# A fused attention and mixture-of-experts kernel: v in the layout of k and q, a new order of the attention steps, and the routed stage written out as an ordered list

## The chip, the cores and the metric

The kernel runs on one core of a Trainium2 chip. The metric is device time in microseconds (us) of one execution, as the median of three runs. Five engines work beside each other: TensorE (PE; its weight loads are shown apart as PEld), VectorE (DVE), ScalarE (ACT), GpSimd (POOL) and SyncE (SP), which here only issues DMAs.

## The reference

The output of an attention layer goes through two mixture-of-experts layers. Inputs are random, in float32.

```python
# attention: 4 batches, 8 heads, S = 576, head size 64
scores = q @ k.T / 8 + bias          # bias: a small MLP of relative positions, one table per head
attn = exp(scores - max); attn = attn / (sum(attn) + 1e-9)
x = (attn @ v) with heads side by side       # 2304 tokens x 512

# soft MoE: 8 experts with 4 slots each, w1 512x1024, w2 1024x512
logits = x @ phi                     # 2304 x 32
d = softmax of logits over tokens;   slot_in = d.T @ x        # 32 x 512
slot_out[e] = relu(slot_in[e] @ w1[e]) @ w2[e]
x = (softmax of logits over slots) @ slot_out                 # rank 32

# routed MoE: one expert per token, for tokens with x @ w_skip > 0
e = argmax(x @ w_gate); g = its softmax weight
out = x + g * (relu(x @ w1[e]) @ w2[e])
```

After the soft MoE each token is a mixture of 32 slot outputs, x = cT . S4, and the mixing weights cT are kept instead of x. The kernel expects that all routed tokens choose one expert; `code` says whether that holds, and a slower loop stands behind it if it doesn't.

## The kernel before

**Attention** is done in 16 pairs n (two heads, one batch), each in five row tiles t of queries: four of 128 rows, t = 4 being the 64 rows left of both heads. A pair's steps are named in a table. LK, LQ and LV load k, q and v (L333, L338, L346); BA and BM load tiles of the position bias. KHI/KLO and QHI/QLO (GpSimd) split k and q into a high and a low part of reduced precision. KG, QG and LAST transpose them on TensorE (suffix p) and copy them out (suffix e, ScalarE). SW (L423, GpSimd) makes a second copy of k with its halves swapped. QKtj (L451 to L461) makes the scores `sc` of tile t and head j on TensorE, its eviction (L468, VectorE) adds the bias and takes the extreme value `st`, EXtj (L475, ScalarE) the exponential e. For tiles 0 to 2, HI (L486, GpSimd) and LO (L490, VectorE) split e into two float16 halves in a tile `ehl`, and TD (L495) has a DMA issued by SyncE transpose it into eT; AVtj (L576, L580) multiplies eT with v. Tiles 3 and 4 are transposed on TensorE (T3, T4) and multiplied by AVB (L588). For v, LV loads tn with an overlapping access: each partition holds eight rows of 64 numbers of both heads, in two DMAs; VA (L382, L386) copies them, scaled, into tv: one copy of 512 columns over all partitions and two of 64 columns over half of them, for the ninth rows; VH and VLO make its float16 halves v16. N0, N1, NB and N3 divide by the sums and write X, XT and XU transpose it, LG adds to the logits `lgT` (LG, in every second pair, and SA, SB, SC in the last four are the soft MoE's logits and slot sums).

What sets the order: under `manual_schedule` each engine runs its instructions in the order in which the code issues them. The code sorts all steps of all pairs by `n * II + SCHED[step]`, with II = 14100, and by `LAST[step]` in the last four pairs, and issues them in this order, so each engine, and SyncE's queue, has its part of the sorted list. A number of the table reaches the chip only through this order. Sorting starts after the bias tables and a few early steps; the first load in it waits for the last bias load (`lead`).

**The stream.** When the last transpose is issued, SyncE issues the loads of the soft experts' weights (`weight_piece`, L239 and L244, 64 pieces of 512 KB) into a ring of buffers; TensorE multiplies each as it lands. At piece 24 of the second half the kernel guesses the routed expert and loads its weights w1e and w2e, in four quarters each. `w10` holds gate and skip weights; `rk` a table of constants.

**The routed stage** is one straight run of code. It multiplies cT by SW for the gate logits (L1143), and VectorE takes from them the maximum, the mask and the counts of tokens per expert (`cnt`), which TensorE sums (L1153). `slots` (L1070) and `slots_sum` (L1078) multiply the slots' outputs with w1e, `bounds` (L1178) finds for each hidden unit whether it can be positive at all, `x2(t)` (L1092, L1093) writes x of tile t, one product and one copy by ScalarE or VectorE, in nineteen turns. The units that can change sign, at most 128, are gathered: a gather reads their rows of w2 (`W2c`), and `Gc` holds their first layer. The buffers `pg` and `py` hold four PSUM tiles each.

**The last loop** (L1298 to L1308) takes the 18 tiles in groups of four (4, 0, 1, 2, 3): `hid(g)` makes the hidden values of a group, one product (L1275), hhi on ScalarE (L1276) and hlo on VectorE (L1277); it is called one group ahead, before the tiles of the present group. Each tile has four products into y (L1302 to L1305), one addition on VectorE (L1306) and a store in two halves (L1350), one issued by SyncE, one by ScalarE.

Of the kernel before, what the change touches and what calls it, by code (L numbers as in the profile page):

```python
# [20 lines left out]
P = 128  # L21
# [14 lines left out]
SCHED = {"LK": 0, "LQ": 6481, "LV": 18003, "BA": 29213, "BM": 40002, "TD0": 37159, "TD1": 48797, "TD2": 38491,  # L36
         "KHI": 4821, "KLO": 9101, "QHI": 9252, "QLO": 10704, "VA": 21547, "VH": 33628, "VLO": 35392, "KG0p": 14818,
# [11 lines left out]
LAST = {"LK": [1362, -2225, -531, 82], "LQ": [1402, 4025, 6684, 922], "LV": [13529, 24916, 14702, 18622],  # L49
         "BA": [16706, 42343, 32163, 20903], "TD0": [38203, 45142, 33962, 21822], "TD1": [56442, 46262, 35002, 22702],  # L50
         "TD2": [42582, 45222, 33442, 21302], "KHI": [2606, 6011, 10736, 15262], "KLO": [4960, 9316, 11410, 15302],
         "QHI": [7495, 7003, 13862, 15622], "QLO": [11336, 11842, 13902, 15782], "VA": [25094, 28402, 30002, 19382],
# [53 lines left out]
def soft_moe_attention_kernel(ctx, tc, q, k, v, w1, b1, w2, phi, mw1, mw2,  # L106
# [139 lines left out]


    qm_b = [fix.tile([P, 4, 64], F32R, name=f"qm{i}") for i in range(2)]
    tv_b = [fix.tile([P, 5, 2, VD], F32, name=f"tv{i}") for i in range(2)]
    for t in qm_b:  # L250
        pool.memset(t.bitcast(F32), 0.0)
    for t in tv_b:
        pool.memset(t[:, 0:4], VS)
        pool.memset(t[:, 4], 0.0)
        for j in range(2):
            pool.memset(t[j * 64:(j + 1) * 64, 4, j, 64:VD], VS)
# [1148 lines left out]
```

## Time and profile before

| what | value |
| --- | --- |
| three runs: median (lowest to highest) | 488.33 us (487.57 to 489.01) |
| the profiled execution, its own time; its span | 484.54 us; 482.8 us |
| busy, share of the span: PE, DVE, ACT, POOL | 419.8 (87%), 349.5 (72%), 304.9 (63%), 248.0 (51%) us |
| PEld | 309.0 us (64%) |
| DMA | 112.02 MB, 232 GB/s in the mean |
| chain that ended last, by engine | PE 43%, DMA 30%, DVE 7%, ACT 7%, POOL 6% |
| its largest single item | the transposing DMA eT<-ehl, 16% |

The span is the time from the first to the last recorded instruction. Busy times are means over stages with different limits. The chain is followed back from the last instruction, at each step to what released it. A mean granted clock of TensorE of 1.0 is full speed (2.4 GHz), 0.50 is its lower level (1.2 GHz).

### The profile page before, as it was taken

How to read it: one execution, taken by the hardware profiler on the slowest of the kernel's cores; microseconds unless marked ns; L12 is line 12 of the kernel's file. 1: busy time of each engine (PE TensorE's matmuls, PEld its weight loads, DVE VectorE, ACT ScalarE, POOL GpSimd, SP SyncE). 2: the span in 40 equal slices, each digit the busy share in tenths (PEclk: the TensorE clock that was granted, in tenths of full speed). 3: DMA queues.
4: the chain of work that ended last, by engine and by line, in shares of the span. 5: the costliest groups of instructions: out<-in, count | busy, mean ns of one | idle time of the engine just before them, and what ended most of it. 6: DMA issues, size and time to landing. Idle time of an engine off the chain costs nothing.

```text
span 482.8 us, 11572 instructions
## 1 busy us (share of the span) xinstructions
PE 419.8 (87%) x4314; PEld 309.0 (64%) x4314; DVE 349.5 (72%) x825; ACT 304.9 (63%) x635; POOL 248.0 (51%) x243
## 2 busy tenths in 40 slices
PE   4789996999989989979989999987887687989993
PEld 2445666998878978878988878876453211355462
DVE  6999966898896988868979788997564600147564
ACT  3999966988896988868888787874421200037510
POOL 5530018898996997995998799853300000000000
PEclk9989997999998999989999999999999799979998
DMA  6468859999999999999899999689999999890166
GB/s 187 151 217 276 281 189 208 238 209 236 193 224 243 171 216 226 216 197 220 205 210 245 176 194 198 148 152 204 390 392 411 403 394 400 304 330 0 28 202 196
DMA packets 151997, 112.02 MB, mean 232 GB/s; under 512 B 118176, under 2 KB 120736, under 8 KB 151936
## 3 DMA queue, kind: packets, MB, share of 16 engines
q1 hardware_dynamic: 150032, 107.99, 86.5%
q10 hardware_dynamic: 1824, 2.97, 1.8%
q8 instruction: 36, 0.59, 0.5%
q0 software_dynamic: 80, 0.26, 0.2%
q14 instruction: 25, 0.20, 0.1%
HBM read 67.49 MB, written 15.34 MB: 172 GB/s over the span
## 4 chain that ended last, share of the span: by engine, by line
PE 43%; DMA 30%; DVE 7%; ACT 7%; POOL 6%; issue 4%; SPq 1%; ACTq 0%; POOLq 0%; DVEq 0%
DMA eT<-ehl 16%; PE sc L451 8%; PE sc L208 8%; DMA x<-in_moe_w_dram 6%; PE av L580 4%; DMA k<-in_moe_w_dram 2%; DMA bias<-in_moe_w_dram 2%; DVE ehl L490 2%; PE pt L406 2%; DVE xnat L1306 2%; ACT ev L211 2%; POOL k L423 2%; PE av L576 2%; PE pbig L1030 2%; PE pt L686 2%
## 5 line engine op out<-in xcount | busy, mean ns | idle before, releaser
L468 DVE CUSTOM_DVE_ANT_0 e<-sc,bias 128x576 f32<-128x576 f32 x128 | 92.5, 750 | 19.1 <-PE sc L451 18.7
L451 PE MATMUL sc<-k,qT 128*128 128x288 f32 x512 | 97.5, 321 | 7.0 <-DVE st L468 4.8
L475 ACT ACTIVATE e<-e,st 128x576 f32<-128x576 f32 x128 | 96.8, 774 | 6.4 <-DVE st L468 5.8
L486 POOL TENSOR_SCALAR ehl<-e 128x1152 f16<-128x1152 f32 x48 | 63.7, 1331 | 71.1 <-ACT e L475 68.4
L490 DVE SCALAR_TENSOR_TENSOR ehl<-e,ehl 128x1152 f16<-128x1152 f32 x48 | 85.1, 1773 | 5.1 <-POOL ehl L486 5.1
L451 PEld LDWEIGHTS sc<-k,qT 128*128 128x128 f32 x512 | 74.7, 196 | 13.7 <-DVE st L468 7.9
L208 PE MATMUL sc<-hid,w2b 128*32 128x288 f32 x576 | 52.5, 434 | 6.5 <-ACT ev L211 3.7
L204 DVE TENSOR_SCALAR hid<-ll,nib 128x576 f32<-128x576 f32 x117 | 55.6, 557 | 1.4 <-PE sc L208 1.4
L580 PE MATMUL av<-v,eT 128*128 128x65 f16 x1152 | 49.9, 195 | 0.0
L423 POOL TENSOR_SCALAR k<-k 64x1152 fp32r<-64x1152 f32 x30 | 47.2, 1575 | 3.8 <-ACT k L439 1.8
L208 PEld LDWEIGHTS sc<-hid,w2b 128*32 128x32 f32 x576 | 27.5, 114 | 29.4 <-ACT ev L211 12.8
L580 PEld LDWEIGHTS <-eT 128*128 128x128 f16 x1152 | 44.2, 99 | 1.5 <-issue 0.3
L371 POOL TENSOR_SCALAR sk<-tk 128x576 fp32r<-128x576 f32 x16 | 30.4, 1899 | 10.4 <-PE pt L434 4.8
L211 ACT ACTIVATE ev<-sc,offs,ipi 128x576 f32<-128x576 f32 x36 | 29.8, 828 | 6.9 <-PE sc L208 6.6
L588 PE MATMUL av<-eq,tv 128*64 128x192 f32 x320 | 29.5, 331 | 0.0
L1132 POOL TENSOR_SCALAR Lt<-rk 128x128 f16<-128x128 f32 x1 | 0.3, 297 | 56.7 <-DMA sk<-in_moe_w_dram 56.7
L576 PE MATMUL av<-v,eT 128*128 128x130 f16 x144 | 16.5, 224 | 14.3 <-DMA eT<-ehl 14.3
L543 PE MATMUL pt<-ident,e 128*128 128x128 f32 x144 | 24.4, 281 | 2.0 <-ACT e L475 2.0
L997 DVE COPY part<-pbig 128x256 f32<-128x256 f32 x2 | 0.8, 425 | 33.0 <-ACT part L996 33.0
L588 PEld LDWEIGHTS av<-eq,tv 128*64 128x64 f32 x320 | 21.6, 137 | 3.7 <-issue 0.5
L996 ACT COPY part<-pbig 128x256 f32<-128x256 f32 x2 | 0.7, 372 | 36.6 <-PE pbig L1030 36.6
L548 ACT COPY eq<-pt 128x512 f32<-128x512 f32 x32 | 18.7, 586 | 8.0 <-PE pt L543 7.6
(338 smaller groups left out, 883.2 us busy)
## 6 DMA issues: line engine op xcount, KB each, us to landing
scratch<-ev SPq DMA_DIRECT2D x36, 288.0 KB, 3.7
x<-in_moe_w_dram SPq DMA_DIRECT2D x20, 512.0 KB, 10.2
bias<-scratch SPq DMA_DIRECT2D x16, 576.0 KB, 5.2
bias<-in_moe_w_dram SPq DMA_DIRECT2D x17, 512.0 KB, 10.3
tn<-in_v_dram SPq DMA_DIRECT2D x32, 256.0 KB, 5.5
k<-in_moe_w_dram SPq DMA_DIRECT2D x16, 512.0 KB, 10.5
tk<-in_k_dram SPq DMA_DIRECT2D x16, 288.0 KB, 3.1
tq<-in_q_dram SPq DMA_DIRECT2D x16, 288.0 KB, 5.7
```

The lines of the kernel that those rows point to most:

```text
L204: vec.tensor_scalar(out=hid, in0=src, scalar1=nib[:, gi:gi + 1], scalar2=None, op0=ALU.max)
L208: pe.matmul(pb[c * 32:(c + 1) * 32, hh, 0:288], lhsT=w2b, rhs=hid[:, hh * 288:(hh + 1) * 288], start=True, stop=True)
L211: act.activation(ev, pb[:, :, 0:288].rearrange("p a (l u) -> p u a l", u=NU), AF.Identity, bias=offs[not on_act], scale=ipi[:, bt:bt + 1])
L371: pool.tensor_scalar(out=sx[:, :, 0, :], in0=t, scalar1=1.0, scalar2=1.0, op0=ALU.mult, op1=ALU.mult)
L423: pool.tensor_scalar(out=k1[64 * i:64 * i + 64], in0=k0[64 - 64 * i:128 - 64 * i], scalar1=1.0, scalar2=1.0, op0=ALU.mult, op1=ALU.mult)
L451: pe.matmul(sc[:, hh, 0:288], lhsT=l_, rhs=kf[i][:, o:o + 288], start=(i == 0), stop=(i == 1))
L468: vec.tensor_tensor_reduce(out=z["e", t][:, o].rearrange("p (a j) -> p a j", a=2), in0=z.pop(("sc", t, j))[:, :, 0:288], in1=bias_t[hp, t] ...
L475: act.activation(ee, ee, AF.Exp, bias=z["m", t][:, j:j + 1], scale=-1.0, **kw)
L486: pool.tensor_scalar(out=eh[:, 0], in0=z["e", t], scalar1=ES, scalar2=1.0, op0=ALU.mult, op1=ALU.mult)
L490: vec.scalar_tensor_tensor(out=eh[:, 1], in0=z.pop(("e", t)), scalar=ES, in1=eh[:, 0], op0=ALU.mult, op1=ALU.subtract)
L580: pe.matmul(av[:, oj:oj + VD], lhsT=eT[:, ei, 5 * j + c], rhs=v16[:, vi, c, j], start=False, stop=lastt and k_ == 2 and c == 3)
L588: pe.matmul(z["av", 1][j * 64:(j + 1) * 64, o], lhsT=tv[:, c, j, 0:64], rhs=z["eq"][:, 4 * j + c if c < 4 else 8], start=False, stop=last ...
```

## The change

**v.** LV loads v like k and q: one DMA, nine rows of 64 numbers of one head in each partition, 64 partitions for each head. `tv` has ten blocks instead of five times two; VA fills it with four copies over 64 partitions each, two of five rows (320 columns) and two of four (256 columns). VH, VLO and the AV products only index it anew.

```diff
-    tv_b = [fix.tile([P, 5, 2, VD], F32, name=f"tv{i}") for i in range(2)]
+    tv_b = [fix.tile([P, 10, VD], F32, name=f"tv{i}") for i in range(2)]
...
         def LV():
-            tn = new(v_p, [P, 2, 8, 64], F32, "tn", bufs=1)
-            src = v[b, h0, 0, :]
-            for a in range(2):
-                sync.dma_start(out=tn[a * 64:(a + 1) * 64].rearrange("p j u d -> p j (u d)"),
-                               in_=bass.AP(tensor=src.tensor, offset=src.offset + a * 64,
-                                           ap=[[NU * 64, 64], [S * 64, 2], [1, 512]]))
+            sync.dma_start(out=new(v_p, [P, NU, 64], F32, "tn"),
+                           in_=v[b, h0:h0 + 2].rearrange("h (l u) d -> (h l) u d", u=NU))
...
         def VA():
-            tn = z["tn"][:, 0, 0, :]
-            act.activation(tv[:, 0:4, :, 0:64], bass.AP(tensor=tn.tensor, offset=tn.offset,
-                                                        ap=[tn.ap[0], [2 * 64, 4], [9 * 64, 2], [1, 64]]), AF.Copy, scale=VS)
             for j in range(2):
-                i, o = slice(64 - j * 64, 128 - j * 64), slice(j * 64, (j + 1) * 64)
-                act.activation(tv[o, 4, j, 0:64], z["tn"][i, j, 7 - 7 * j], AF.Copy, scale=VS)
+                i, o = slice(j * 64, (j + 1) * 64), slice(64 - j * 64, 128 - j * 64)
+                act.activation(tv[i, 5 * j:5 * j + 5, 0:64], z["tn"][i, 0:NU:2], AF.Copy, scale=VS)
+                act.activation(tv[o, 6 * j:6 * j + 4, 0:64], z["tn"][i, 1:NU:2], AF.Copy, scale=VS)
...
-                    pe.matmul(av[:, oj:oj + VD], lhsT=eT[:, ei, 5 * j + c], rhs=v16[:, vi, c, j],
+                    pe.matmul(av[:, oj:oj + VD], lhsT=eT[:, ei, 5 * j + c], rhs=v16[:, vi, 6 * j + c],
```

**The order of the attention steps.** SCHED and LAST have new numbers throughout; II stays. The entries that are spoken of below:

| step | before | after | | step | before | after |
| --- | --- | --- | --- | --- | --- | --- |
| LQ | 6481 | 0 | | LO0 | 31998 | 29204 |
| LK | 0 | 1320 | | AV00 | 38684 | 41620 |
| LV | 18003 | 1698 | | LO1 | 40817 | 36350 |
| BA | 29213 | 28833 | | AV10 | 49644 | 45586 |
| BM | 40002 | 37041 | | LO2 | 34798 | 28988 |
| TD0 | 37159 | 37204 | | AV20 | 41201 | 38306 |
| TD1 | 48797 | 37353 | | KLO | 9101 | 7086 |
| TD2 | 38491 | 37080 | | KG0p | 14818 | 10835 |

The order on SyncE's queue for one pair of the middle, before (the start of a row is the line, then the operation and its tiles; "bias2" is one of the bias buffers, "ehl" the two halves of a row tile). The three transposes are those of row tiles 1, 0 and 2:

```order
L333 DMA tk_2488<-in_k_dram 128x576
L269 DMA bias2_2503<-scratch_72 128x1152
L346 DMA tn_2549<-in_v_dram 64x2x512 x2
L338 DMA tq_2593<-in_q_dram 128x576
L495 DMA_TRANSPOSE eT_2595<-ehl_2379 128x18x128
L495 DMA_TRANSPOSE eT_2668<-ehl_2505 128x18x128
L495 DMA_TRANSPOSE eT_2690<-ehl_2530 128x18x128
```

and after:

```order
L344 DMA tq_2513<-in_q_dram 128x576
L275 DMA bias2_2518<-scratch_72 128x1152
L339 DMA tk_2534<-in_k_dram 128x576
L349 DMA tn_2547<-in_v_dram 128x576
L495 DMA_TRANSPOSE eT_2690<-ehl_2475 128x18x128
L495 DMA_TRANSPOSE eT_2692<-ehl_2480 128x18x128
L495 DMA_TRANSPOSE eT_2696<-ehl_2561 128x18x128
```

q has gone to the front and v is one load; the transposes still stand in a row behind the loads, now in the order of row tiles 2, 0 and 1.

**The routed stage.** Each piece of code becomes a named step, with the PSUM tile of each kept in a dictionary, and a string `ORDER` says in which order they are issued. w10 moves to another pool, and the product of ST4 with w10 (PW) becomes a step of the stage.

```diff
+ORDER = ("SL0 PW SL1 GP0 SS0 SWt GP1 P4 SW SS1 PL0 GH0 BD0 PL1 S4t SD0 S4 GH1 BD2 SD1 X17 RR2 GB0 PL2 X3 SL2 "
+         "XE17 PL3 GP2 RR0 SL3 SS2 XE3 GP3 MX GB1 BD3 EX GH2 X4 ACTM EA CNT RR3 XE4 LG8 SS3 BD4 SD2 GB2 GH3 X11 "
...
+         "XE9 X5 PN M9 C9 PR EX2 MR2 HOE SLA EXP SLB GE1 YOA PIA FL X10 XE10 PIB POSM GS1 GCE IX EIDX X15 ELIST "
+         "XE5 YOB GS2 GACT GC X13 XE15 X6 GCF MISC PT X0 XE13 YT X7 GATH XE6 BAD XE7 H4 H0 TP H4A H4D W2CH P4B "
+         "X16 W2CL T4T XE16 T4 X18 H0A XE18 PO H0D X12 XE12 XE0 ACCO")
+X2V = (7, 18)
...
-        w10 = sp.tile([P, 4, 10], F32, name="w10")
+        w10 = late.tile([P, 4, 10], F32, name="w10")
...
+    def x2e(t):
+        (vec.tensor_copy if t in X2V else act.copy)(acc[:, t, :] if t < NT else accO, z.pop(("x2", t)))
```

SL, GP, SS, GH, SD and GB are the parts of `slots`, `slots_sum` and `slots_low`; PL the gate products; MX, EX, EA and CNT VectorE's way to the counts, PN their product; BD and RR the bounds and their maxima; X and XE the products and copies of x2, two of the copies on VectorE where there were four. TensorE's order at the start of the stage, before ("pc" and "y" are PSUM tiles, "bias_5706" is ST4):

```order
L1001 MATMUL pc<-sel,part_6329 128x128 x4
L1043 MATMUL pw<-w_6296,bias_5706 128x10 x4
L1140 MATMUL pc<-ident,bias_5706 128x128 x4
L1143 MATMUL y<-SW,bias_6218 128x10 x8
L1143 MATMUL y<-SW,w 128x10 x10
L1143 MATMUL y<-SW,cO 128x10
L1070 MATMUL pc<-w1e,bias_5706 32x256 x4
L1153 MATMUL y<-cnt,ones 128x8
L1070 MATMUL pc<-w1e,bias_5706 32x256 x4
L1078 MATMUL pc<-gp,sel 128x256
L1070 MATMUL pc<-w1e,bias_5706 32x256 x4
```

and after:

```order
L1000 MATMUL pc<-sel,part_6327 128x128 x4
L1070 MATMUL pc<-w1e,bias_5716 32x256 x4
L1157 MATMUL pc<-w_6294,bias_5716 128x10 x4
L1070 MATMUL pc<-w1e,bias_5716 32x256 x4
L1078 MATMUL pc<-gp,sel 128x256
L1167 MATMUL pc<-ident,bias_5716 128x128 x4
L1078 MATMUL pc<-gp,sel 128x256
L1176 MATMUL y<-SW,bias_6216 128x10 x5
L1216 MATMUL pc<-MR,gh 128x512
L1176 MATMUL y<-SW,bias_6216 128x10 x3
L1176 MATMUL y<-SW,w 128x10 x2
L1216 MATMUL pc<-MR,gh 128x512
```

The slots' products with w1e now come first, the gate products follow in four pieces, and the product of cnt (L1153 before) is no longer among them: counted from the last product with `part` it was the 7th row and is the 35th.

**The last loop.** `hid` is cut in three, `hid_p` (the product), `hid_a` (hhi) and `hid_d` (hlo); for groups 4 and 0 all three stand in ORDER (H4, H4A, H4D, H0, H0A, H0D). The products and hhi of a group are called two groups ahead, hlo behind the second tile of a group.

```diff
-            for g in (4, 0, 1, 2, 3):
-                if g != 3:
-                    hid((g + 1) % 5)
+            groups = (4, 0, 1, 2, 3)
+            for i, g in enumerate(groups):
+                ahead = groups[i + 2] if i < 3 else None
+                if i < 3:
+                    hid_p(ahead)
+                    hid_a(ahead)
                 for t in range(4 * g, min(4 * g + 4, NT)):
...
                     store((sync, act), out, acc, t)
+                    if i < 3 and t % 4 == 1:
+                        hid_d(ahead)
```

ScalarE's order as it enters the loop, before:

```order
L1093 COPY xnat<-y 128x512 x6
L1291 TENSOR_LOAD code
L1292 COMPARE_AND_BRANCH
L1276 ACTIVATE hhi<-pc 128x512
L1350 DMA out_dram<-xnat 64x512 x2
L1276 ACTIVATE hhi<-pc 128x512
L1350 DMA out_dram<-xnat 64x512 x4
L1276 ACTIVATE hhi<-pc 128x512
```

and after:

```order
L1327 ACTIVATE hhi<-pc 128x512
L1103 COPY xnat<-y 128x512 x2
L1356 TENSOR_LOAD code
L1357 COMPARE_AND_BRANCH
L1327 ACTIVATE hhi<-pc 128x512
L1419 DMA out_dram<-xnat 64x512 x2
L1327 ACTIVATE hhi<-pc 128x512
L1419 DMA out_dram<-xnat 64x512 x4
```

In the loop before, the rows are hhi of group 0, two stores of group 4, hhi of group 1, four stores of group 0, hhi of group 2. After, hhi of group 0 stands in the routed stage, and hhi of group 1 ahead of the stores of group 4, that of group 2 ahead of those of group 0: each is one group further ahead of its tiles.

## Rows read from the trace of the kernel before

**Rows 1.** Busy time by stretch (us; instructions in brackets), granted clock, DMA share, GB/s.
```profile
core 0: us, PE busy (x) PEld busy (x) DVE busy (x) ACT busy (x) POOL busy (x), PEclk, DMA share, GB/s
104.20:255.70 151.50, 139.94 (x1661) 125.89 (x1660) 127.30 (x306) 124.64 (x275) 131.29 (x109) 0.98 1.06 214
255.70:336.60 80.90, 72.62 (x880) 63.10 (x878) 70.27 (x168) 61.65 (x138) 61.24 (x52) 1.00 0.94 185
336.60:420.20 83.60, 67.78 (x579) 28.02 (x581) 29.11 (x75) 13.72 (x37) 4.96 (x25) 0.96 1.03 390
424.10:455.10 31.00, 28.61 (x165) 15.40 (x164) 19.70 (x58) 17.15 (x39) 3.19 (x9) 0.89 0.33 117
455.10:476.20 21.10, 18.70 (x76) 13.95 (x76) 14.71 (x22) 3.49 (x7) 0.00 (x0) 1.00 0.59 180
```

**Rows 2.** The same view, three single attention pairs.
```profile
154.70:170.50 15.80, 15.77 (x193) 14.49 (x192) 14.39 (x34) 14.33 (x32) 14.01 (x12) 1.00 0.98 183
170.50:187.30 16.80, 14.87 (x183) 13.17 (x183) 13.95 (x36) 13.40 (x31) 15.06 (x13) 1.00 1.12 230
203.10:223.20 20.10, 17.36 (x194) 15.73 (x192) 14.23 (x34) 14.01 (x32) 14.95 (x13) 0.92 1.13 234
```

**Rows 3.** TensorE's waits, 104.2 to 255.7 us: total, times, longest.
```profile
PE av L576 <- DMA eT<-ehl: 9.3, 6, 2.7
PE sc L451 <- POOL k L423: 1.2, 1, 1.2
PE sc L451 <- DVE st L468: 0.7, 1, 0.7
```

**Rows 4.** The tile eT: who waited, and DMA time to landing.
```profile
  PE av L576: 14.3, 12
DMA to landing us min/median/max: 4.5/5.3/9.5
```

**Rows 5.** Timeline of SyncE's queue: start, us, line, tiles, count.
```profile
204.21 12.59 SPq L495 DMA_TRANSPOSE eT<-ehl  x3
216.89 0.54 SPq L333 DMA_DIRECT2D tk<-in_k_dram  x1
217.48 0.41 SPq L269 DMA_DIRECT2D bias<-scratch  x1
218.00 1.29 SPq L346 DMA_DIRECT2D tn<-in_v_dram  x2
219.39 0.54 SPq L338 DMA_DIRECT2D tq<-in_q_dram  x1
223.25 3.39 SPq L495 DMA_TRANSPOSE eT<-ehl  x1
```

**Rows 6.** The tile tn: ScalarE's copies, min/median/max ns, count and shapes.
```profile
L386 ACT ACTIVATE tv<-tn x32: 254/256/260, 11.6 to 317.4; 64x64 f32<-64x64 f32 x32
L382 ACT ACTIVATE tv<-tn x16: 617/633/644, 11.0 to 316.4; 128x512 f32<-128x512 f32 x16
```

**Rows 7.** DMA issues: KB each, median us to landing.
```profile
bias<-scratch SPq DMA_DIRECT2D x16, 576.0 KB, 5.2
tn<-in_v_dram SPq DMA_DIRECT2D x32, 256.0 KB, 5.5
tk<-in_k_dram SPq DMA_DIRECT2D x16, 288.0 KB, 3.1
```

**Rows 8.** Routed stage: the stretch of low clock; the wait before it.
```profile
429.20:435.40 6.20, 5.80 (x31) 2.45 (x31) 4.16 (x18) 2.56 (x7) 0.40 (x1) 0.50 0.70 269
429.60 0.60 PE L1153 MATMUL y<-cnt,ones 128*128 128x8 f32 x2 [0.98 <-DVE cnt L1149]
```

**Rows 9.** Last loop: ScalarE's and VectorE's instructions, idle time before in brackets.
```profile
464.57 0.60 ACT L1276 ACTIVATE hhi<-pc 128x512 fp32r<-128x512 f32 x1 [4.17 <-DMA out_dram<-xnat]
...
L1306 DVE SCALAR_TENSOR_TENSOR xnat<-y,mskm,xnat 128x512 f32<-128x512 f32 x18 | 12.3, 744 | 0.1
L1277 DVE SCALAR_TENSOR_TENSOR hlo<-pc,hhi 128x512 fp32r<-128x512 f32 x4 | 2.8, 692 | 6.9 <-ACT hhi L1276 6.9
```

More of the change, by code (lines that the diff above doesn't have):

```diff
@@ L1040, in soft_moe_attention_kernel @@
         vec.tensor_copy(st4[:, 256:512], pt[1][:, 0:256])
-        pw = p1.tile([P, 10], F32, name="pw")
-        for kc in range(4):
-            pe.matmul(pw, lhsT=ST4[:, kc, :], rhs=w10[:, kc, :], start=(kc == 0), stop=(kc == 3))
-        SWt = late.tile([P, 10], F32R, name="SWt")
         ctl = ExitStack()
         ctl.enter_context(tc.manual_schedule(engines=fixed))
-        act.copy(SWt, pw)
-        vec.scalar_tensor_tensor(out=SW, in0=SWt, scalar=lom, in1=pw, op0=ALU.mult, op1=ALU.add)
     wctx.close()
@@ new lines, in PW @@
+        @part
+        def PW():
+            z["pw"] = pg.tile([P, 512], F32, name="pc")
+            for kc in range(4):
+                pe.matmul(z["pw"][:, 0:10], lhsT=ST4[:, kc, :], rhs=w10[:, kc, :], start=(kc == 0), stop=(kc == 3))
+        step["SWt"] = lambda: act.copy(SWt, z["pw"][:, 0:10])
+        step["SW"] = lambda: vec.scalar_tensor_tensor(out=SW, in0=SWt, scalar=lom, in1=z.pop("pw")[:, 0:10],
+                                                      op0=ALU.mult, op1=ALU.add)
+        @part
@@ new lines, in P4, with gates @@
+        def P4():
+            z["p4"] = pg.tile([P, 512], F32, name="pc")
+            for kc in range(4):
+                pe.transpose(z["p4"][:, kc * P:(kc + 1) * P], ST4[:, kc, :], ident)
+        step["S4t"] = lambda: act.copy(S4t, z["p4"])
+        step["S4"] = lambda: vec.scalar_tensor_tensor(out=S4, in0=S4t, scalar=lom, in1=z.pop("p4"), op0=ALU.mult, op1=ALU.add)
+        def gates(i):
+            if i == 0:
+                z["pl"] = py.tile([P, 512], F32, name="y")[:, 0:NA * 10].rearrange("p (t x) -> p t x", x=10)
+            for t in range(5 * i, min(5 * i + 5, NA)):
+                pe.matmul(z["pl"][:, t, :], lhsT=cT(t) if t < NT else cO, rhs=SW, start=True, stop=True)
@@ L1181, in g_T, with bounds_max @@
+        def bounds_max(f):
+            vec.tensor_reduce(out=rr[:, f], in_=z.pop(("pb", f)).rearrange("p (i n) -> p i n", i=2), axis=AX.X, op=ALU.max)
+        each(" ".join(f"BD{f}" for f in range(8)), bounds)
+        each(" ".join(f"RR{f}" for f in range(8)), bounds_max)
         def g_T(hf):
-            pt = py.tile([P, 4, P], F32R, name="y")
+            pt = z["gt", hf] = py.tile([P, 4, P], F32R, name="y")
             for i in range(4):
@@ L1226, in soft_moe_attention_kernel, with PH @@
-        vec.scalar_tensor_tensor(out=mr, in0=pr[:, 0:8], scalar=1.0, in1=m9[:, 0:8], op0=ALU.add, op1=ALU.mult)
-        for hf in range(2):
+        each("GT0 GT1", g_T)
+        each("GE0 GE1", lambda hf: act.copy(GT[:, 4 * hf:4 * hf + 4, 0:P], z.pop(("gt", hf))))
+        @part
+        def PH():
+            hv = z["ph"] = pg.tile([P, 512], F32, name="pc")[:, 0:8 * NO].rearrange("p (f n) -> p f n", f=8)
+            for f in range(8):
+                pe.matmul(hv[:, f], lhsT=G[:, f * P:(f + 1) * P], rhs=cO[:, 0:NO], start=True, stop=True)
@@ L1228, in soft_moe_attention_kernel, with places @@
+        def places(hf):
             f = slice(4 * hf, 4 * hf + 4)
@@ new lines, in soft_moe_attention_kernel, with picked @@
+        each("YOA YOB", left_out)
+        step["YT"] = lambda: act.copy(yt, z.pop("yO"))
+        def picked(i):
+            if i == 0:
+                z["pi"] = pg.tile([P, 512], F32, name="pc")
+            for f in range(4 * i, 4 * i + 4):
+                pe.matmul(z["pi"][:, 0:P + 2], lhsT=Sl[:, f], rhs=GT[:, f], start=f == 0, stop=f == 7)
+        each("PIA PIB", picked)
+        step["GS2"] = lambda: vec.tensor_tensor(out=GS, in0=GS, in1=posm.unsqueeze(2).to_broadcast([P, 8, NSL]), op=ALU.mult)
@@ new lines, in PT, with GC @@
+        @part
+        def PT():
+            z["pT"] = pg.tile([P, 512], F32, name="pc")
+            for f in range(8):
+                pe.matmul(z["pT"][f % 4 * 32:(f % 4 + 1) * 32], lhsT=GS[:, f], rhs=w2e[:, f], start=f < 4, stop=f > 3)
+        step["TP"] = lambda: act.copy(Tp, z.pop("pT"))
+        @part
+        def GC():
+            z["gc"] = pg.tile([P, P], F32R, name="pc")
+            pe.transpose(z["gc"], GcT, identr)
+        step["GCF"] = lambda: act.copy(Gc, z.pop("gc"))
+        @part
```

304 lines of the change are left out of this document (140 added, 164 removed), and 105 rows, old and new, of tables (LAST, ORDER, SCHED).

## The prediction, made before the changed kernel ran

> **What bounds the kernel now.** I read the stretches first, then the waits inside the one that is longest, then single instructions. The program falls into five stretches [rows 1]. Up to 64.7 us the bias tables are made (no part of the change works there). From 64.7 to 336.6 us sixteen attention pairs run, 271.9 us. From 336.6 to 420.2 us the dense expert weights stream in: the DMA engines are busy for 1.03 of the time at 390 GB/s, and TensorE only follows. From 424.1 to 455.1 us the routed stage works out its tables, and from 455.1 to 476.2 us its last loop adds eighteen tiles and stores them.
>
> In attention the reader is to see that no engine has much room. In the nine pairs between 104.2 and 255.7 us, 16.83 us each, TensorE is busy 139.94 of 151.5 us, the others 124 to 132, the DMA engines 1.06 [rows 1]. Two kinds of pair lie under this mean. Where no transposed tile comes late, a pair takes 15.8 us, TensorE 15.77 of them: there it is the bound [rows 2]. The pair of 203.1 to 223.2 us takes 20.1, with TensorE idle 2.7 us and a mean granted clock of 0.92 [rows 2]. What TensorE waits for in the nine pairs is almost one thing: the transposed weights eT, 9.3 of 11.2 us, in 6 waits; over the whole program 14.3 us in 12 [rows 3, 4].
>
> Why eT is late is seen on SyncE's queue [rows 5]. It issues the three transposes of a pair in a row, 12.59 us here, then k, bias, two pieces of v, and q until about 219.9; the next transpose is issued at 223.25. A transpose lands 5.3 us after its issue in the median, but up to 9.5 [rows 4]; the one issued at 204.21 us, 0.1 us behind q's load, is such a late one. So lateness goes with what stands directly ahead of the transpose.
>
> **The change, part by part: v.** The load falls from 32 DMAs of 256 KB to 16 of 288 KB [rows 7]: 8.2 MB become 4.6 MB. At the 214 GB/s that this stretch moves [rows 1], the 3.6 MB are 16.7 us of queue time, 1.05 us per pair, and SyncE is spared one issue per pair. It is no gain by itself: TensorE waits for transposes, and it counts through them, below.
>
> ScalarE made tv with one copy of 512 columns, 633 ns, and two of 64 columns, 256 ns each [rows 6], 1.15 us. The four new copies have 320, 256, 320 and 256 columns. No row has these shapes; between the two, a column costs (633-256)/448 = 0.84 ns, so they are 471 and 417 ns, together 1.78 us: 0.63 us per pair more, 10.1 us in all. ScalarE has room: it is busy 124.64 of 151.5 us, 13.8 per pair; with 0.63 it comes to 14.5, below TensorE's 15.8. I take 0; 10.1 us is the cost if ScalarE were on the path in each pair.
>
> **The new attention order.** The counts and shapes of TensorE's work are the same, so its busy time is the floor: 15.77 us in a pair with logits (193 matmuls), 14.87 in one without (183) [rows 2], 15.3 in the mean. What moves is the distance between a transpose and its user. In table units (one pair is 14,100 units, measured 16.83 us), the low half LO is followed by its AV product after 6,686, 8,827 and 6,403 units for row tiles 0, 1 and 2 now, and 12,416, 9,236 and 9,318 after. On SyncE the transpose right behind the loads was that of tile 1, and is that of tile 2, so for this one the distance grows only from 8,827 to 9,318, 0.6 us. But what stands ahead of it is smaller (1.44 MB for 1.66, [rows 7]), which is the 1.05 us again, and it stands there sooner: the last load's turn comes 7,964 units after the start of tile 1's low half now (q, 48,781 against 40,817), and 910 after that of tile 2 then (v, 29,898 against 28,988). For this I take 1 us, an estimate between nothing and the 3.0 us that the loads took on the queue in the row. Together 2.6 us against stalls of up to 2.7: most go, thin ones stay, above all in the pairs that load the mixed bias tile, which now stands just ahead of the transposes.
>
> So of 9.3 us in these nine pairs I take two thirds, 6.2 us. The clock gives something back: the mean of 0.98 over 151.5 us [rows 1] is 3.0 us at stake; I take 2.0. Outside these pairs, I take nothing for the last four, whose order is wholly new. Against it stand waits that a new order must bring: VectorE's evictions of scores now follow two low halves in a row, and KLO comes 3,749 units ahead of KG0p instead of 5,717; the nearest rows are the waits of 1.2 us for GpSimd's k copy and 0.7 us for VectorE [rows 3], and I take 1.2 us. Attention: -6.2 - 2.0 + 1.2 = -7.0 us. Bounds: the best is all idle time and clock of the nine pairs and the same share of the other seven, 9 x (16.83 - 15.3) = 13.8 us, and some 3 more, -17; the worst is the slower rival.
>
> The stream of weights follows the last transpose on SyncE, and is as long as before, so what attention gains goes to the end undiminished. The three small loads that change places in it (w10 and rk) cost nothing there.
>
> **The routed stage.** Between 424.1 and 455.1 us TensorE is busy 28.61 of 31.0 us, but from 429.2 to 435.4 us at a granted clock of 0.50, its lower level of 1.2 GHz [rows 1, 8]. Before it fell the engine had waited for VectorE's counts, 1.0 us [rows 8]: the gate chain (maximum, mask, counts) stood ahead of everything. In the new order weight products, P4 and bounds fill that place, and the counts' product is the 35th row behind the last transposing product instead of the 7th. Its own work stays the same. So the ceiling is the idle 2.4 us and half of 5.80 us at the lower clock, 2.9 us: 5.3 us. I take 4.0, since nineteen copies still have to empty four buffers and the first product now needs the first quarter of w1e just as it lands. If the clock falls all the same it is 1 to 2 us.
>
> **The last loop.** ScalarE's queue issues half of the stores, and a store waits for VectorE. So hhi of the next group stands behind four stores (4.17 us idle), hlo on VectorE waits for it, and four tiles' additions wait for hlo: 6.9 us of waits in three turns and the entry [rows 9]. Now hhi is made two groups ahead and hlo between the tiles. Then TensorE bounds: 18.70 us for 76 matmuls [rows 1], 75 of them are 18.5, and one addition of 0.7 us is left behind: 19.2 for 21.1, 1.9, say 2.0 us. It is covered as long as VectorE needs less: 12.3 + 2.8 us [rows 9] for 18.5. What follows the last addition stays.
>
> **Sum.** The profiled execution took 484.54 us (a span of 482.8 and 1.7 around it). 484.54 - 7.0 - 4.0 - 2.0 = 471.5. The runs' median is 488.33, 3.79 above, so 475.3.
>
> **The rivals.**
> *Attention does not gain.* The five engines need 13.8 to 15.6 us per pair; with ScalarE's 0.63 and a transpose still behind the loads, the pairs stay at 16.8. For it: the distance of that transpose grows by 0.6 us only. Then 488.33 - 6 = 482.3. Chance 0.20.
> *All stalls go.* -14 in attention, -6 behind: 468. For it: the pairs of 15.8 us exist now. Chance 0.14.
> *Slower: the transposes behind four loads.* All three transposes of a pair now stand behind q, bias, k and v, and the mixed bias where there is one; if tile 2's transpose is late, tiles 0 and 1 are late after it. Price: a pair like that of 203.1 us takes 20.1, 3.3 over the mean. It decides once more than two pairs more than now are of this kind, since 2 x 3.3 eats the 6 us of the routed stage; with every second of 14 it is +23 - 6, 505 us. Against it: three of the four loads' turns come by the table a good while before the low halves. Chance 0.11. The Trainium skill, in "DMA: Bandwidth & Descriptors" under "Queues, rings and completion order", says that descriptors on an engine are consumed in ring order; by that rule tile 2's transpose waits for all 1.44 MB ahead of it, which is this rival and its time. The late landing behind loads agrees (up to 9.5 us for a median of 5.3).
> *It cancels out.* Pairs of 17.3 us instead of 16.83 eat the 6 us: within 0.3%. Chance 0.05.
>
> **How the numbers follow.** The forecast has 0.50, its own range is 470 to 480. Faster by over 0.3% (1.5 us, about the spread of the three runs) are the forecast and the first two rivals, 0.84; same 0.05; slower 0.11. The range holds the forecast, the first rival and most of the second: 466 to 485.5.
>
> **What would show it.** Right: TensorE's waits for eT over the program fall from 14.3 to 5 us or less; the pairs of the middle stretch take 15.8 to 16.3 us; the routed stage shows no stretch at 0.50 and takes 27 us; in the loop, hhi no longer waits for stores. Wrong: eT waits as long as now on the transpose behind v; a new long wait for scores or KLO; the stream of weights starting later than 332 us (329.6 by the sum); a low clock after 424 us. The forecast fails if attention keeps its 271.9 us, or if the order of the last four pairs, which I priced at nothing, loses or gains several us.

## The result, and the profile after

The changed kernel took 472.86 us, the median of four runs (470.75 to 474.76), the kernel before 487.95 us beside it (484.94 to 489.01): a ratio of 0.970, interval 0.964 to 0.976. Two later runs of the same code, on two different chips, gave 473.25 us (0.980, 0.975 to 0.985) and 471.66 us (0.974, 0.970 to 0.977). The changed kernel hardly moves between the three; the kernel before does, with times from 479.1 to 491.4 us over all runs. Ratios compare undisturbed runs alone, and so do the times of the kernel before that are given beside e1 to e12; a ratio is not always the quotient of the medians. The profiled execution of after took 474.76 us with a span of 472.5.

The first view is the busy time by stretch of after, cut at the same events as [rows 1] where these exist: nine attention pairs, the rest of attention up to the first piece of the weight stream, the stream, the routed stage from the last product with `part` to the loop's first product, and the loop to its last addition.

```profile
core 0: us, PE busy (x) PEld busy (x) DVE busy (x) ACT busy (x) POOL busy (x), PEclk, DMA share, GB/s
110.06:255.69 145.63, 140.28 (x1671) 124.08 (x1671) 131.60 (x307) 128.59 (x285) 135.18 (x109) 1.00 0.96 208
255.69:329.33 73.64, 69.14 (x834) 60.31 (x832) 65.29 (x158) 60.18 (x134) 57.73 (x50) 1.00 0.92 179
329.33:421.03 91.70, 75.53 (x600) 29.22 (x598) 29.66 (x79) 14.34 (x39) 5.39 (x29) 0.91 0.98 360
421.03:447.75 26.72, 26.61 (x175) 16.37 (x175) 18.98 (x58) 18.33 (x43) 2.95 (x5) 1.00 0.42 147
447.75:466.24 18.49, 17.65 (x75) 13.53 (x73) 15.60 (x24) 2.74 (x5) 0.00 (x0) 1.00 0.69 206
```

Nine pairs take 145.63 us, 16.18 each, where they took 16.83, at a clock of 1.00 [rows 1]. The first piece of the stream goes out at 329.33 us instead of 336.61. The stream is longer: 91.70 us from its first piece to the last product with `part`, where before, cut in the same way, it is 86.3 (336.61 to 422.95). From there to the loop's first product it is 26.72 us for 32.5, with no stretch at 0.50 [rows 8], and the loop takes 18.49 us for 20.7, both cut in the same way.

The second view is TensorE's waits in the nine pairs (total, times, longest), and two rows on the tile eT, over the program.

```profile
PE pt L543 <- DVE xnat L650: 2.4, 5, 0.5
PE pt L543 <- DVE rs L610: 1.5, 4, 0.4
PE sc L451 <- DVE st L468: 1.0, 4, 0.3
PE av L576 <- DMA eT<-ehl: 0.2, 1, 0.2
```

```profile
  PE av L576: 1.6, 2
...
DMA to landing us min/median/max: 4.5/5.2/8.8
```

Waits for eT are nearly gone: 0.2 us for 9.3 [rows 3], over the program 1.6 for 14.3 [rows 4]. In their place stand short waits for the transposing buffers (L543, behind VectorE's normalization). What the new copies of v cost, against the 633 and 256 ns of [rows 6]:

```profile
L385 ACT ACTIVATE tv<-tn x32: 455/469/476, 10.1 to 310.8; 64x320 f32<-64x320 f32 x32
L386 ACT ACTIVATE tv<-tn x32: 415/417/420, 10.6 to 311.3; 64x256 f32<-64x256 f32 x32
```

In the last loop ScalarE and VectorE show this (idle time before in brackets, and the group's in the last column):

```profile
451.12 0.60 ACT L1327 ACTIVATE hhi<-pc 128x512 fp32r<-128x512 f32 x1 [1.82 <-PE y L1373]
...
457.32 0.60 ACT L1327 ACTIVATE hhi<-pc 128x512 fp32r<-128x512 f32 x1 [5.60 <-DMA out_dram<-xnat]
```

```profile
L1332 DVE SCALAR_TENSOR_TENSOR hlo<-pc,hhi 128x512 fp32r<-128x512 f32 x4 | 2.7, 684 | 0.1
```

One hhi still stands 5.60 us behind stores, as before [rows 9], but hlo waits 0.1 us in all instead of 6.9: nobody needs that hhi yet.

### The profile page after: what moved, and what is told of

The parts are those of the page before. It is cut to its first block, busy times and chain, and to the rows that moved or that the text cites. A ratio compares the mean times of both kernels' runs of the same rounds, so it can differ in the third digit from the quotient of the medians.

```text
span 472.5 us, 11520 instructions
## 1 busy us (share of the span) xinstructions
PE 422.3 (89%) x4314; PEld 309.9 (66%) x4314; DVE 352.8 (75%) x824; ACT 312.6 (66%) x652; POOL 253.2 (54%) x241
## 5 line engine op out<-in xcount | busy, mean ns | idle before, releaser
L468 DVE CUSTOM_DVE_ANT_0 e<-sc,bias 128x576 f32<-128x576 f32 x128 | 94.6, 749 | 13.7 <-PE sc L451 12.5
L490 DVE SCALAR_TENSOR_TENSOR ehl<-e,ehl 128x1152 f16<-128x1152 f32 x48 | 87.4, 1839 | 0.8 <-POOL ehl L486 0.6
L486 POOL TENSOR_SCALAR ehl<-e 128x1152 f16<-128x1152 f32 x48 | 57.9, 1215 | 12.5 <-ACT e L475 10.9
L423 POOL TENSOR_SCALAR k<-k 64x1152 fp32r<-64x1152 f32 x30 | 57.5, 1915 | 3.4 <-ACT k L439 0.7
L215 PEld LDWEIGHTS sc<-hid,w2b 128*32 128x32 f32 x576 | 29.4, 114 | 27.5 <-ACT ev L218 10.6
L394 POOL TENSOR_TENSOR v<-tv,v 128x650 f16<-128x650 f32 x16 | 22.9, 1431 | 41.0 <-ACT v L390 41.0
L543 PE MATMUL pt<-ident,e 128*128 128x128 f32 x144 | 25.0, 286 | 4.4 <-DVE xnat L650 2.4
L375 POOL TENSOR_TENSOR sq<-tq,sq 128x576 fp32r<-128x576 f32 x16 | 24.1, 1506 | 0.3
L375 POOL TENSOR_TENSOR sk<-tk,sk 128x576 fp32r<-128x576 f32 x16 | 22.7, 1420 | 0.2
## 6 DMA issues: line engine op xcount, KB each, us to landing
bias<-in_moe_w_dram SPq DMA_DIRECT2D x17, 512.0 KB, 10.5
```

The source lines that it names most:

```text
L215: pe.matmul(pb[c * 32:(c + 1) * 32, hh, 0:288], lhsT=w2b, rhs=hid[:, hh * 288:(hh + 1) * 288], start=True, stop=True)
L375: pool.tensor_tensor(out=z[name][:, :, 1, :], in0=t, in1=z[name][:, :, 0, :], op=ALU.subtract)
L423: pool.tensor_scalar(out=k1[64 * i:64 * i + 64], in0=k0[64 - 64 * i:128 - 64 * i], scalar1=1.0, scalar2=1.0, op0=ALU.mult, op1=ALU.mult)
L468: vec.tensor_tensor_reduce(out=z["e", t][:, o].rearrange("p (a j) -> p a j", a=2), in0=z.pop(("sc", t, j))[:, :, 0:288], in1=bias_t[hp, t] ...
L486: pool.tensor_scalar(out=eh[:, 0], in0=z["e", t], scalar1=ES, scalar2=1.0, op0=ALU.mult, op1=ALU.mult)
L490: vec.scalar_tensor_tensor(out=eh[:, 1], in0=z.pop(("e", t)), scalar=ES, in1=eh[:, 0], op0=ALU.mult, op1=ALU.subtract)
```

## The experiments

In every trace the same four events were read: the issue of the stream's first piece, the last product with `part`, the loop's first product and its last addition. The table has the first as a time, the others as distances from the event ahead; all in us, with the median of the runs. The kernel before took 483.1 us beside e1 to e4, 482.8 beside e5 to e8 and 485.1 beside e9 to e12; these three sets ran on three chips, so times of different sets are compared with care. "Old" and "new" are the order of the attention steps and v's layout.

| run | order | v | first piece at | stream | routed | loop | median |
| --- | --- | --- | --- | --- | --- | --- | --- |
| before | old | old | 336.6 | 86.3 | 32.5 | 20.7 | 487.95 |
| e2, routed stage and loop alone | old | old | 336.2 | 87.7 | 26.7 | 18.5 | 477.59 |
| e3, loop alone | old | old | 333.7 | 87.1 | 32.5 | 18.5 | 483.23 |
| e10, v alone | old | new | 325.9 | 86.5 | 31.7 | 20.8 | 474.63 |
| e1, attention alone | new | new | 330.0 | 87.5 | 32.6 | 20.7 | 478.42 |
| after | new | new | 329.3 | 91.7 | 26.7 | 18.5 | 472.86 |
| e4, after again | new | new | 328.4 | 88.2 | 26.7 | 18.5 | 473.25 |
| e12, after, third time | new | new | 329.4 | 88.6 | 26.7 | 18.5 | 471.66 |
| e5, after with the old loop | new | new | 328.3 | 89.9 | 26.7 | 20.9 | 473.43 |
| e6, counts early | new | new | 329.0 | 89.7 | 31.1 | 18.5 | 476.98 |
| e11, filler products | new | new | 329.6 | 89.4 | 26.7 | 18.5 | 471.98 |
| e8, AV of tile 2 sooner | new, AV2 moved | new | 336.8 | 89.7 | 26.7 | 18.5 | 479.92 |
| e9, one buffer for tn | new | new, one buffer | 346.0 | 91.3 | 26.7 | 18.5 | 488.01 |
| e7, v as before | new | old | 359.4 | 89.6 | 26.7 | 18.5 | 500.43 |

**The parts alone: e1, e2, e3.** Each takes some pieces of the diff and leaves the rest as before.

> The attention part of the change alone (v's layout and the new numbers of SCHED and LAST); routed stage and last loop as before. Theory A (the three parts are worth what the two profiles show, and the stream of weights only follows): the first piece of the stream goes out at 329 to 330 us instead of 336.6, TensorE's waits for eT fall from 14.3 to under 3 us, and the whole is 7 us faster than before, 0.985. Theory B (what attention gains is partly lost in the stream, because the stream's buffers wait for the end of the last pair, which moved less than the first piece did): the first piece goes out as early, but the stream takes 3 us or more longer than before and the whole is only 2 to 4 us faster, 0.992 to 0.996.

e1: 0.991 (0.988 to 0.995), and waits for eT of 1.6 us. The first piece goes out 6.6 us sooner; of these some 4 arrive. The stream is 1.2 us longer than in the trace of before: theory A's time, 0.985, lies just outside the interval, and theory B's loss in the stream is there but smaller than the 3 us it said.

> The routed stage and the last loop of the change alone; v and the order of the attention steps as before. Theory A: worth 5.8 us in the routed stage and 2.2 us in the loop, 8 us together, 0.984; no stretch of the routed stage at a granted clock of 0.50. Theory B (the routed stage was only faster because the clock was by chance high in that execution): the routed stage shows a stretch at 0.50 and the whole is 3 to 5 us faster, 0.990 to 0.994.

e2: 0.990 (0.984 to 0.995). The two stages are shorter by 5.8 and 2.2 us and the clock is 1.00 throughout the routed stage, so theory A holds for where the time goes; of these 8.0 us the runs show 5 with an interval of 2.3 to 7.6, so not all of them arrive. In its trace the stream is 1.4 us longer than in that of before.

> Only the last loop of the change: the product and hhi of a group two groups ahead, hlo behind the second tile; those of group 0 stand near the end of the routed stage, which is otherwise as before. Theory A: hhi no longer waits for stores, the eighteen tiles take 18.5 us instead of 20.7 from the first product to the last, and the whole is 2 us faster, 0.996. Theory B (the stores' landing ends the program, not the additions): the loop's additions end 2 us sooner, but the last store lands as late, and the whole is the same within 0.5 us.

e3: 0.999 (0.995 to 1.003). The loop takes 18.5 us, 2.2 less, in the trace; the runs of before spread too widely to show it.

**The loop undone: e5.** H0, H0A and H0D leave ORDER, and the loop goes back:

```diff
-                if i < 3:
-                    hid_p(ahead)
-                    hid_a(ahead)
+                if i < 4:
+                    for f_ in (hid_p, hid_a, hid_d):
+                        f_(groups[i + 1])
...
-                    if i < 3 and t % 4 == 1:
-                        hid_d(ahead)
```

> The changed kernel with the last loop as before: product, hhi and hlo of a group one group ahead, together, behind the stores; the rest as after. The times of the kernel before spread too widely to show 2 us, those of the changed kernel do not. Theory A: 2.2 us slower than the changed kernel (472.9 and 473.25 us so far), 475.3, and the loop from its first product to its last addition takes 20.7 us instead of 18.5. Theory B (the loop is hidden behind the stores, as the loop alone on the kernel before seemed to say, 0.9991): 473 us.

The time is theory B's, the loop theory A's: it is back at 20.9 us, and VectorE again waits for hhi:

```profile
L1332 DVE SCALAR_TENSOR_TENSOR hlo<-pc,hhi 128x512 fp32r<-128x512 f32 x4 | 2.8, 691 | 5.1 <-ACT hhi L1327 5.1
```

The median of 473.43 us (473.04 to 474.75) is only 0.2 to 1.8 us above the three medians of the changed kernel. So the loop's 2.2 us are shown in each trace, and that all of them reach the time is not.

**The counts moved to the front again: e6.**

```diff
-ORDER = ("SL0 PW SL1 GP0 SS0 SWt GP1 P4 SW SS1 PL0 GH0 BD0 PL1
...
+ORDER = ("SL0 PW SL1 GP0 SS0 SWt GP1 P4 SW PL0 PL1 PL2 PL3 MX ACTM EX EA CNT SS1 PN FL ELIST GH0 BD0 "
...
```

> The changed kernel with the gate products and VectorE's way to the counts moved to the front of the routed stage, directly behind SW, and the counts' product right behind the second slot sum; all other steps keep their order. Theory A (the late counts are the gain, because TensorE no longer stops for them and its clock does not fall): TensorE waits 1 us or more for the counts, the granted clock falls to 0.50 behind the wait, and the routed stage takes 30 to 32 us instead of 26.7, the whole 476 to 478 us. Theory B (the gain lies in the searched order of the rest, the x2 products and copies between the slots): the stage stays within 1 us of 26.7 and the whole at 473 to 474 us.

Theory A's numbers, all of them. The rows are TensorE's wait for the counts and the stretch behind it (busy times by engine, clock):

```profile
427.19 0.60 PE L1191 MATMUL y<-cnt,ones 128*128 128x8 f32 x2 [1.01 <-DVE cnt L1186]
```

```profile
427.00:433.00 6.00, 5.50 (x25) 2.71 (x25) 3.10 (x8) 1.81 (x4) 0.80 (x2) 0.50 0.38 139
```

A stop of 1.01 us, then 6 us at 0.50, as in [rows 8]; the stage takes 31.1 us, 4.4 more, and the whole 476.98 us, some 4 more. TensorE is idle for 1.4 us of the stage instead of 0.1 and busy for 29.7 instead of 26.6. Of the 5.8 us that the new order of the stage brings, 4.4 hang on this one place.

That the stop is what brings the low clock, as theory A says, is not shown, and a trace with the old stage speaks against it. In e3 the clock falls 2 us ahead of the wait for the counts (columns as above, then TensorE's row):

```profile
424.33:425.33 1.00, 1.00 (x11) 1.00 (x11) 0.00 (x0) 0.00 (x0) 0.00 (x0) 1.00 1.10 385
425.33:427.33 2.00, 2.00 (x14) 1.15 (x13) 0.89 (x4) 0.00 (x0) 0.00 (x0) 0.50 1.07 411
```

```profile
427.91 0.60 PE L1153 MATMUL y<-cnt,ones 128*128 128x8 f32 x2 [0.54 <-DVE cnt L1149]
```

In the trace of before it falls as the wait begins, at 428.57 and 428.62 us. In e1 and e6 it falls 0.4 us after the wait began, in e10 0.4 us after it ended, and there the low stretch lasts 3.4 us instead of 6.8. In all five the gate products, 19 of 10 columns each, stand in one row, and run or have run less than 2 us before when the clock falls; in the kernels with the stage as changed, where it stays at 1.00, they are spread out. e6 puts this row and the early wait back together; which of them brings the low clock, no run separates.

**v's layout taken back, and one buffer: e7, e9.** e7 has the changed kernel's order with LV, VA, tv and the AV indices as before. e9 has everything as changed but for one word:

```diff
-            sync.dma_start(out=new(v_p, [P, NU, 64], F32, "tn"),
+            sync.dma_start(out=new(v_p, [P, NU, 64], F32, "tn", bufs=1),
```

> The changed kernel with v loaded and copied as before (two DMAs of 256 KB with the overlapping access, three ScalarE copies); the new order of the attention steps stays. Theory A (the order makes the transposes come in time, by the distance between LO and AV): TensorE's waits for eT stay under 4 us over the program, the middle pairs take 16.2 us, and the whole is within 1 us of the changed kernel, 472 to 474 us. Theory B (the 3.6 MB of v that are no longer moved make the room in which the transposes land in time): the waits for eT come back to 8 us or more and the whole is 4 to 6 us slower, 477 to 479 us.

e7 was to leave v's bytes alone in question, and was slower than the kernel before: 500.43 us, 1.030 (1.025 to 1.036). Theory B named the right sign, and neither the size nor the reason. SyncE's and TensorE's waits in e7, 104 to 250 us:

```profile
SPq L353 <- ACT tv L393: 35.4, 8, 5.9
```

```profile
PE av L583 <- DMA eT<-ehl: 14.4, 9, 2.9
```

In the table of after, LV (1,698 + 14,100 = 15,798) stands ahead of the copies VA of the pair before it (18,073); before, it stood behind them (18,003 against 21,547 - 14,100 = 7,447). With the old tile's single buffer, v's load has to wait for these copies, and behind it on SyncE's queue stand the three transposes.

> The changed kernel with one buffer for tn instead of two; layout, bytes and copies of v and the order of the steps as changed. Theory A (the order issues v's load ahead of the copies of the pair before, so it needs the second buffer, and with one SyncE's queue stands still in front of the transposes): SyncE waits 30 us or more for ScalarE's copies of v, TensorE's waits for eT are 14 us or more, and the whole is at 498 to 502 us, as with v's old layout. Theory B (the old layout was slow for its bytes and its overlapping access): within 1 us of the changed kernel, 472 to 474 us.

The same wait with the new layout; SyncE's waits, and its queue in one pair:

```profile
SPq L349 <- ACT tv L386: 40.0, 8, 6.3
```

```profile
160.16 0.38 SPq L339 DMA_DIRECT2D tk<-in_k_dram  x1
164.74 0.33 SPq L349 DMA_DIRECT2D tn<-in_v_dram  x1
165.16 9.66 SPq L495 DMA_TRANSPOSE eT<-ehl  x3
```

From 160.16 to 164.74 us the queue stands. e9 takes 488.01 us, 1.005 (1.002 to 1.008), 16 more than e12 beside it: theory A's mechanism (waits for eT are 16.6 us over the program) with a smaller price. What e7 loses beyond that, 1.030 for 1.005 or some 12 us, belongs to the old layout in this order. So the new order needs the second buffer of tn. Two buffers of the old tile, which is 4 KB per partition for 2.3, were not tried.

**The distance: e8.**

```diff
-         ... "BM": 37041, "TD0": 37204, "TD1": 37353, "TD2": 37080,
+         ... "BM": 34990, "TD0": 37204, "TD1": 37353, "TD2": 35000,
...
-         ... "AV20": 38306, "AV21": 39019,
+         ... "AV20": 35306, "AV21": 36019,
```

> The changed kernel with the AV products of row tile 2 issued 3,000 table units (3.4 us) sooner, so that 6,318 units lie between its low half LO and its AV product instead of 9,318 (6,403 before the change); on SyncE's queue the transposes, loads and bias tiles stand in the same order in the middle pairs. Theory A (the distance between LO and its AV product is what keeps TensorE from waiting): waits for eT rise from under 2 to 6 us or more, nearly all at the transposes of tile 2, and the whole is 2 to 6 us slower, 475 to 479 us. Theory B (what counts is that the last load's turn on the queue comes sooner): waits for eT stay under 3 us and the whole is at 473 us.

The time is theory A's or just over it, 479.92 us, 0.986 (0.981 to 0.991), some 7 us slower than after; the waits are theory B's. Rows on eT, and TensorE's largest wait:

```profile
  PE av L576: 1.6, 2
...
DMA to landing us min/median/max: 4.6/5.2/8.4
```

```profile
PE sc L457 <- DVE st L468: 6.6, 8, 0.9
```

With no more distance than before the change, eT still comes in time. In the traces too: over eight middle pairs tile 2's AV product starts 6.9 us after the end of its low half in e8, 8.9 us in after, 7.6 in before. TensorE now stops eight times at the scores of the 64 left-over rows; that the moved AV products had filled the time until VectorE emptied the score buffer is an argument from the order, not a test. For row tile 2 the distance between LO and AV is not what made the transposes come in time; e8 leaves those of tiles 0 and 1 long.

**v alone: e10.** The kernel before with the new LV, tv, VA, VH and AV indices, and the old tables.

> The kernel before with v's new layout, load, buffers and four copies alone; the order of all steps as before. Theory A (the layout gains nothing by itself, since the transposes keep their place): waits for eT of 12 to 15 us and a ratio of 0.997 to 1.003. Theory B (3.6 MB less let the transposes land sooner): waits for eT under 10 us and 3 to 5 us faster, 0.990 to 0.994. Theory C (ScalarE's 0.63 us more per pair fall on the path, 10.1 us at most): 1.005 to 1.02.

Theory B, and by more than it said: 0.980 (0.976 to 0.983). Busy time of nine pairs in e10 and the rows on its eT:

```profile
104.85:246.32 141.47, 138.21 (x1663) 124.27 (x1663) 127.92 (x306) 129.68 (x285) 135.67 (x109) 1.00 1.02 216
```

```profile
  PE av L569: 4.3, 6
...
DMA to landing us min/median/max: 4.5/5.1/7.2
```

A pair takes 15.72 us, TensorE is busy for 15.36 of them, at a clock of 1.00: in these pairs TensorE is the bound. Waits for eT fall from 14.3 to 4.3 us and the longest landing from 9.5 to 7.2. The first piece of the stream goes out at 325.9 us, sooner than in any kernel with the new order. e1 differs from e10 in the tables alone, and is slower: 0.991 for 0.980, intervals apart, though on another chip. On e10's own chip e12 takes only 3.0 us less, 471.66, with a routed stage and a loop that are 7.4 us shorter: some 4 us are lost ahead of them. In e1, after, e4 and e12 the new order with the new v brings the first piece to 328.4 to 330.0 us, some 3.4 later than e10; the three traces with the old order and the old v have it at 333.7 to 336.6. Where v's layout acts is seen at row tile 1, whose transpose stands right behind the loads in the old order: over eight middle pairs it lands 7.5 us after its issue in before and 6.3 in e10, while the distance from low half to AV product is shorter in e10, 7.2 us for 8.3. In after this transpose is the last of the three and takes 5.2 us. In the old order v's load never waits for the copies, so the second buffer has no part in e10; whether the bytes, the one DMA for two or the way in which they lie in memory does it, no run separates.

**The stream's first products: e4, e11, e12.**

> The changed kernel again, unchanged, for a second profile. In the first, TensorE's granted clock fell to 0.50 for 349 to 354 us, while it worked off the first pieces of the stream, and the stream took 91.7 us from its first piece to its last product, 86.3 before. Theory A (that fall is a matter of the single execution): here the clock stays at 1.00 there, the stream takes 86 to 89 us, and the span is 469 to 470 us. Theory B (the new order of the last four pairs brings the fall): the fall is here too, and the stream again takes 91 to 92 us. The time against before: 0.970.

> The changed kernel with three products of 256 columns added on TensorE in front of the last product of the slot sums, where it stands still for 0.9 us just before the first pieces of the stream are worked off; nothing uses their result. Theory A (that stop brings the fall of the granted clock to 0.50 behind it, and the slower products free the stream's buffers late): the clock is over 0.90 in the first 5 us of these products instead of 0.53 to 0.78, the stream's 21st piece lands 32 to 33 us after the first was issued instead of 33 to 36.5, and the whole is 1 to 2 us faster than the changed kernel beside it. Theory B (the fall has another cause): the clock falls again, and the whole is the same or 0.5 us slower.

> The changed kernel a third time, for a time on the same chip as the three runs beside it: 473 us, with a span of 468 to 473 us; the stream from its first piece to its last product 88 to 92 us.

e11 puts three products of `sel` with a piece of x ahead of the step FSp:

```diff
+            for i in range(3):
+                pe.matmul(z["pfs"][:, 256:512], lhsT=sel, rhs=X[0][:, 0, 0:256], start=True, stop=True)
```

The same nine microseconds, first of after, then of e12, which is the same code (columns as above):

```profile
348.00:351.00 3.00, 3.00 (x19) 2.67 (x18) 0.62 (x3) 0.00 (x0) 0.00 (x0) 0.65 0.44 73
351.00:354.00 3.00, 3.00 (x31) 1.40 (x33) 2.45 (x5) 0.37 (x1) 0.00 (x0) 0.50 1.00 354
354.00:357.00 3.00, 3.00 (x45) 1.51 (x40) 2.49 (x5) 0.31 (x1) 0.00 (x0) 0.72 0.85 254
```

```profile
348.00:351.00 3.00, 2.77 (x49) 1.97 (x50) 2.81 (x7) 0.00 (x0) 0.00 (x0) 1.00 0.99 281
351.00:354.00 3.00, 3.00 (x63) 2.19 (x56) 2.09 (x6) 0.68 (x1) 0.00 (x0) 1.00 1.01 363
354.00:357.00 3.00, 3.00 (x47) 1.65 (x41) 1.28 (x3) 0.80 (x2) 0.00 (x0) 1.00 1.00 382
```

In after TensorE works at 0.50 to 0.72 while it has to empty the stream's first buffers, and the DMA engines are busy for as little as 0.44 of the time; in e12 the clock is 1.00 and they go on. e4 has the fall in part (0.72 in the first 5 us of these products, a stream of 88.2 us). So its length is a matter of the single execution, as theory A of e4 said, and it does not belong to the new order: with the old one the clock of these 5 us is 1.00 in before and e2, 0.66 in e3 and 0.73 in e10. The stop ahead of it is not enough to bring it: e12 has the same one, and keeps its clock.

```profile
345.93 0.38 PE L769 MATMUL pt<-fsel,bias 128*128 128x32 f32 x2 [0.91 <-ACT bias L721]
```

e11, which fills this stop, has a clock of 1.00 there and the same time as e12, 471.98 for 471.66 us: theory B. Its 21st piece lands 34.3 us after the first was issued, no sooner than e12's 33.6.

That the stream is longer remains, and the traces show it in two places. Early, with the new order of attention: the 21st piece lands after 33.1 to 36.5 us in ten traces, with the old order after 31.9 to 33.2 in four. Later, with the new routed stage: the twenty pieces from the 25th to the 45th take 26.8 to 28.5 us in the ten kernels that have it, e2 with the old order of attention among them, and 25.9 to 26.3 in the four that have not, e1 with the new order among them. The low clock has a part in the first only: with the old order the 21st piece lands after 31.9 us where the clock stays at 1.00 (before, e2) and after 32.9 and 33.2 where it falls (e10, e3); with the new order it is 33.1 to 34.3 where it stays (e7, e11, e12) and 33.3 to 36.5 where it falls. What makes the rest, and the second, is open.

## Why the prediction was right, and where not

The time, the sign and the size were right: 472.86 us for 475.3, within the likeliest case's own range. The parts that add up to it were right only in part.

**Attention, -7.0: right in size, wrong in its origin.** The first piece was forecast for 329.6 us and went out at 328.4 to 330.0; waits for eT were to fall to 5 us or less and fell to 1.3 to 1.9; pairs of 15.8 to 16.3 us are 16.18. But the step that said of v's load "It is no gain by itself" and gave -6.2 us to the new order failed. e10 shows the opposite: v's layout alone brings the first piece forward by 8 to 11 us, and the new order on top of it takes 3.4 back. That the whole came out near the forecast is in this part luck. The 1.05 us of queue time per pair, which the prediction worked out and then counted as a part of the order's gain, is near what e10 gains per pair, 1.11 us (15.72 for 16.83); that the bytes are the reason is not shown by that. The argument by distance (6,686, 8,827, 6,403 units) fell for tile 2 with e8, and e10 gains without any of it. The prediction's reading that lateness goes with what stands directly ahead of a transpose held (7.5, 6.3 and 5.2 us for tile 1). The Trainium skill, in "DMA: Bandwidth & Descriptors" under "Queues, rings and completion order", has descriptors on an engine consumed in ring order; e10 fits that: with less ahead of the transposes their longest landing falls from 9.5 to 7.2 us. The rival built on that rule, 505 us, did not come in the kernel as it is. The bound of -17 us was summed wrongly: the same share of the other seven pairs, 1.53 us each, is 10.7 us and not 3; what was measured lies inside either.

**What was not seen.** The new order moves v's load ahead of the copies of the pair before. That needs the second buffer of tn, which the edit brings in by leaving out `bufs=1`; without it the gain in attention is lost, at 488 us (e9). The prediction read the diff of LV for its bytes and copies and passed over the buffers.

**The copies of v.** 469 and 417 ns for 471 and 417 estimated; they cost nothing that shows, as taken.

**The clock, -2.0, and new waits, +1.2.** The nine pairs are at 1.00 for 0.98. TensorE's waits for other things than eT are 4.9 us in the nine pairs, 3.0 more than the 1.9 of [rows 3] where 1.2 were taken; e10 has 2.5 of its 3.26 us of idle time. This is part of what the new order costs.

**The stream as long as before: wrong by about 2 us**, as the table shows. Both the new order of attention and the new routed stage have a share in it; whether the move of w10, which was priced at nothing, is behind the second, no run shows.

**The routed stage, -4.0: under-sized.** The stage takes 26.7 us in every trace that has it as changed, for 31.7 to 32.6 with the old one: -5.0 to -5.9, where the ceiling was 5.3. The idle time goes from 2.4 to 0.1 us as the ceiling had it; the busy time from 30.1 to 26.6, 3.5 us where 2.9 were taken for the clock. That the early place of the gate chain costs this is shown by e6. The reading that the engine had waited for the counts before its clock fell does not hold in the trace of before itself, where the fall comes as the wait begins, and less so in e3, where it comes 2 us ahead of it.

**The loop, -2.0:** -2.2 to -2.4 in the traces. That hhi would no longer wait for stores was not so, 5.60 us in after; the gain came all the same, since hlo no longer needs that hhi at once.

Attention -6 to -7, stream +2, routed stage -5.8 and loop -2.2 are -12 to -13 us; in the three sets of runs of the changed kernel the medians lie 10 to 15 below those of before.

## What to carry to other kernels

A change of several parts can have its size forecast and its credit given to the wrong one: one run of the smallest part alone, here v's load, would have told more than the distances in the table. An order and the buffers that it needs are one edit: ask of each load that is moved which reader must have let go of its tile, and what stands behind it on its queue. By these runs the old order with the new v, the routed stage and the loop of after should be the fastest: e10's 474.63 less 5.0 (31.7 to 26.7) and up to 2.3 for the loop is 467 to 470 us, and some 1 us more if the stream slows with the new routed stage as in the ten traces; this is an estimate, and none of the twelve runs tried it.

## What was not expected of the hardware

The same code shows a granted clock of 0.50 to 0.72 in one execution and 1.00 in another over the same nine microseconds (after, e12), with the same stop of 0.9 us ahead. And the pace of the weight stream goes with the program: the twenty pieces from the 25th to the 45th, 10.5 MB with nothing else on the queue, land in 25.9 to 26.3 us in the four kernels with the old routed stage and in 26.8 to 28.5 in the ten with the new one, although these loads stand in the same order; three executions of the changed code agree, 26.8 to 27.0. Why is open.
